# Four interleaved attention layers: VectorE may also take causal score banks

## The chip, the cores and the metric

One core of one Trainium2 chip. The metric is the device time of one execution, in microseconds (us); three executions of the kernel before are known, and one of another execution was recorded by the hardware profiler.

## The reference

Four residual layers on x of 2048 tokens by 512 features, all with 32 heads of 16 features. Layers 0 and 2 ("A") cut the tokens into four segments of 512: causal softmax attention inside each segment, blended by a gate with a read of a memory matrix that the earlier segments have filled. Layers 1 and 3 ("B") are plain attention of all tokens with all tokens.

```python
def _A_ref(x, wq, wk, wv, wo, beta):
    ...
    for s in range(N):                       # N = 4 segments, L = 512 tokens each
        qs, ks, vs = (q[:, :, s].copy(), k[:, :, s].copy(), v[:, :, s].copy())
        logits = jnp.einsum('bhqd,bhkd->bhqk', qs, ks) * scale + mask
        p = _softmax(logits, axis=-1)
        a_dot = jnp.einsum('bhqk,bhkd->bhqd', p, vs)
        pq = phi(qs)
        num = jnp.einsum('bhld,bhde->bhle', pq, M)
        den = jnp.einsum('bhld,bhd->bhl', pq, z)[..., None] + 1e-06
        a_mem = num / den
        o = g * a_mem + (1.0 - g) * a_dot
        outs.append(o)
        pk = phi(ks)
        M = M + jnp.einsum('bhld,bhle->bhde', pk, vs)
        z = z + jnp.einsum('bhld->bhd', pk)
    ...
def _B_ref(x, wqkv, wo):
    ...
    scores = jnp.einsum('bhqd,bhkd->bhqk', q, k) * Dh ** (-0.5)
    p = _softmax(scores, axis=-1)
    o = jnp.einsum('bhqk,bhkd->bhqd', p, v)
    ...
x = A_x
x = x + _A_ref(_layernorm(x, axis=-1), A_wq, A_wk, A_wv, A_wo, A_beta)
x = x + _B_ref(_layernorm(x, axis=-1), B_wqkv, B_wo)
x = x + _A_ref(_layernorm(x, axis=-1), A_wq, A_wk, A_wv, A_wo, A_beta)
x = x + _B_ref(_layernorm(x, axis=-1), B_wqkv, B_wo)
```

## The kernel before

The program is a list of instructions for each engine, made ahead of time by a planner (`Builder`) that walks through steps and keeps an estimate of each engine's time (`Sched`). What follows are the parts that the change and the prediction speak of.

**Banks.** PSUM has eight banks of 128 partitions by 512 fp32 values here. The scores of 128 keys (partitions) by 512 queries of one head fill one bank. In a B layer such a bank takes one matmul (32 rows of KB against a masked copy of the queries, `qm`); it is a full bank. In an A layer the causal triangle leaves ten blocks of 128 by 128 of a head's sixteen, packed in banks by `PARTS`: "k0" is one matmul of 512 columns, "k13" four matmuls of 128 columns (key blocks 1 and 3), and "k2" holds key block 2 of two heads. After the scores of a causal bank, one more matmul adds the mask: `ident` against `tri`, -1e9 above the diagonal, on 128 or 256 columns.

**Groups.** A group is a head in each of four rows of the array for one segment of queries. An A group has 12 banks (its first of a pair, e = 0) or 8 (its mate, e = 1, whose k2 blocks lie in the first's banks). A B group has 64 banks, or 16 or 32 where its keys come in waves. In all there are 640 causal banks and 4096 full ones.

**Units.** In each step `unit` scores the next three banks of the groups in the list `sel`, in order, into banks 0-2 or 3-5 in turn; one ScalarE activation (L1294) takes the exponential of all three into pT. The value matmuls ("pv") follow two units later and gather in bank 6. When all banks of a group are through, `finish` normalizes it (L1346, L1354).

**Bank 7** serves everything else: projections, output projections, the memory's matmuls, and the banks that VectorE takes.

**Taken banks.** In a step `dx_pick` may take one bank out of a group that is still to be scored. Its scores go to bank 7 and VectorE computes their exponential: L934 from PSUM into one half of a space "in" (dxt, later KA and QA too), then for a pair of banks at a time a chain of five instructions (L959, L962, L964, L966, L970) that ends in a space "out" (dxo, later VA too). Early there are two pairs of space in and three out. Once layer 0 is through (`dx_widen`, `self.wide`), its buffers make that four and four. The value matmuls read a taken bank from its out space when its group is the current one, and only then does the space come free. A bank is taken only if the group is a B one, of 64 banks unless much lies ahead (`NEARW`), has not yet given a sixth (wide: a fifth) of its banks, and if from the head of `sel` to its end at least 30 (wide: `REST` = 36) banks are left; a group ahead of the one that gives is shut. Further gates are: `near` (banks of all groups whose projections are done) not below `LOW` = 24; two units between takes, or more while other tasks wait (`ALT3` = 2, `ALT5` = 4); no projection half done; a free space in; bank 7 clear in time; VectorE not too late.

**Background.** Between units the planner runs tasks: layer norms, projections, memory updates, output projections, and the two chain tasks (`task_dx`), within a credit of VectorE time for each unit and while the estimates leave room. `dx_urgent` puts the chains first, and closes a half pair, when a group that has given banks has fewer than 30 (wide: `NEAR` = 24) left. If a group ends with a chain not through, `pv_step` runs the chain at once, in the middle of the unit. `evac` copies a projection out of bank 7 on VectorE, or on ScalarE if the estimate has VectorE more than 500 ns behind. `keep_busy` adds matmuls of zeros where the planner sees too little of TensorE's time in use.

**Order.** The work of layers 0 and 1 runs mixed, then 1 and 2, then 2 and 3: `select` puts a causal pair into `sel` behind the group at the head as soon as its projections are done, full groups behind it.

Of the kernel before, what the change touches and what calls it, by code (L numbers as in the profile page):

```python
# [255 lines left out]

class Builder:
    NPU = 4
    PHI_LATE = 100
    LAG_M = 2  # L260
    LOOK, PV_TAKEN = 1, 1
# [600 lines left out]
    def dx_pick(self, items):  # L862


        if self.low or self.near < self.PAIRS and len(self.dx_pairs) > self.PAIRS2 or self.step - self.dx_step < (2 - self.wide if not self.pending() else self.ALT3 if self.gap > 1 else self.ALT5) or self.cr_dve < -300 and self.late("dve") > self.EARLY or not self.dx_bufs or self.bank_late(self.unit_start()) > self.DX_BANK or self.late("dve") > (self.DX_FIN if self.ends(0) else self.DX_LATE):
            return None
        if any(t["next"][0][:1] == ["cont"] for t in self.tasks):
            return None
        used = {b[1] for _, b in items}
        rest = 0  # L870
        for n, g in enumerate(self.sel):
            rest += len(g.banks) - g.pos
            if g.kind != "B" or g.total < 64 and self.near < self.NEARW or g.shut or g.taken >= g.total // (self.TAKEN if self.wide else 6) or rest < (self.REST if self.wide else 30):
                continue
            for k in range(1, 9):
                if g.banks[-k][1] not in used:
                    bank = g.banks.pop(-k)
                    g.taken += 1
                    self.dx_step = self.step
                    for h in self.sel[:n]:  # L880
                        h.shut = True
                    return g, bank[0], bank[1]
        return None

    def pending(self):
        return any(t not in self.dx_tasks and self.met([n for n in t["next"][0] if n[0] != "at"]) for t in self.tasks)
# [62 lines left out]
    def dx_chain(self, k, b, ents):  # L949


        w = 512 * len(ents)
        ns = (690, 430, 1225) if len(ents) == 2 else (420, 295, 690)
        half = self.dx_space("in", b).bitcast(dt.uint16).rearrange("p (n two) -> p two n", two=2)
        lo, hi = half[:, 0, 0:w], half[:, 1, 0:w]
        z = self.dx_space("z", k)[:, 0:w]
        bt, bz = self.b_dxt[b], [self.b_dxz[k]]
        c = (350, 610, 1150) if self.wide else (440, 710, 1230)
        self.op("dve", lambda e: e.tensor_scalar(z, lo, EXP_K * 2.0 ** -16, EXP_K * EXP_F, op0=ALU.mult, op1=ALU.add), reads=bt,  # L959
                writes=self.dx_writes("z", k, self.b_dxz[k]), ns=ns[0])  # L960
        yield [], 0, c[1]
        self.op("dve", lambda e: e.tensor_tensor(z, z, z, ALU.mult), reads=bz, writes=bz, ns=ns[0])  # L962
        yield [], 0, c[0]
        self.op("dve", lambda e: e.tensor_scalar(z, z, EXP_B, EXP_A, op0=ALU.mult, op1=ALU.add), reads=bz, writes=bz, ns=ns[1])  # L964
        yield [], 0, c[1]
        self.op("dve", lambda e: e.tensor_tensor(z, z, z, ALU.mult), reads=bz, writes=bz, ns=ns[0])  # L966
        yield ["slot"], 0, c[2]
        slot = self.dx_free.pop(0)
        ob = self.dx_space("out", slot).bitcast(dt.int16)[:, 0:w]
        self.op("dve", lambda e: e.scalar_tensor_tensor(ob, hi, 128.0, z, op0=ALU.mult, op1=ALU.add), reads=bt + bz,  # L970
                writes=self.dx_writes("out", slot, self.b_dxo[slot]), ns=ns[2])
        self.dx_bufs.append(b)
        self.dx_now[k] = []
        self.dx_use[slot] = len(ents)
        for i, (g, what, r) in enumerate(ents):
            self.dxq.append((self.step + 2, g, what, r, slot, i))

    def later(self):
        return ("at", self.step + 1)
# [251 lines left out]
    def unit(self, n, items, dx):  # L1231
        u = n % 2
        al = self.new_alloc()
        slot = n % self.NPU
# [29 lines left out]
        if dx is not None:  # L1264
            g, what, r = dx
            bank7, al7 = self.misc(), self.new_alloc()
            rows = slice(32 * r, 32 * r + 32)
            ks, kk = self.kslot(g.L, what // 4), what % 4
            first_mm.append((self.ps[:, bank7.col0:bank7.col0 + 512], self.KB[rows, ks, g.c, kk * 128:(kk + 1) * 128],
                             self.qm[rows, g.qm, :], True, [self.b_KB[ks][g.c], self.b_qm[g.qm]], bank7, r, 512))  # L1270
        for (o, a, q, st, reads, bank, r, N) in first_mm + sum(second_mm, []):
            self.mm(o, a, q, st, True, reads, bank, al7 if dx is not None and bank is bank7 else al, tile=(32, 32 * r, 128, 0), n=N)
        for i, (g, (what, r)) in enumerate(items):
            if g.kind == "A":

                nb = 1 if what == "k0" else 2
                c0 = self.banks[3 * u + i].col0
                self.mm(bcast(self.ps[:, c0:c0 + 1], [[256, nb], [1, 128]]), self.ident[:, :], bcast(self.tri[:, 0:1], [[0, nb], [1, 128]]),
                        False, True, [self.b_ident, self.b_tri], self.banks[3 * u + i], al, n=128 * nb)
        if dx is not None:  # L1280
            self.dx_first(bank7, al7)
            self.dx_build.append(dx)
# [4 lines left out]
        i = 0  # L1287
# [248 lines left out]
```

## Time and profile before

| what | before |
|---|---|
| three executions | 1984.61, 1985.27, 1989.22 us (median 1985.27) |
| the profiled execution: time, span | 1984.7, 1983.0 us |
| granted TensorE clock, mean | 0.996 |
| ScalarE (ACT) busy, of it L1294 | 1933.0 us, 1904.8 us in 1407 instructions |
| VectorE (DVE) busy | 1654.2 us |
| TensorE (PE) busy, weight loads (PEld) | 1700.2 us, 933.7 us |
| banks taken by VectorE (L934) | 517 |

A busy time is the sum of an engine's instructions; matmuls overlap and their ends are modelled, so PE's share is not its share of peak. The slices are fortieths of the span in tenths of busy time. A group of instructions has its line, engine, operation, output<-input, shapes, count, busy time, mean duration, and the idle time of the engine just before them with what ended it. All matmuls have the line of the helper `mm`, so they are told apart by their tensors: ps<-qm,KB scores full banks, ps<-qm,KA causal ones, ps<-tri,ident is the mask, ps<-VB,pT and ps<-VA,pT are the value matmuls, ps<-wB,zero the matmuls of zeros. KA, QA and VA hold taken banks in the later part, beside what their names say.

### The profile page before, as it was taken

How to read it: one execution, taken by the hardware profiler on the slowest of the kernel's cores; microseconds unless marked ns; L12 is line 12 of the kernel's file. 1: busy time of each engine (PE TensorE's matmuls, PEld its weight loads, DVE VectorE, ACT ScalarE, POOL GpSimd, SP SyncE). 2: the span in 40 equal slices, each digit the busy share in tenths (PEclk: the TensorE clock that was granted, in tenths of full speed). 3: DMA queues.
4: the chain of work that ended last, by engine and by line, in shares of the span. 5: the costliest groups of instructions: out<-in, count | busy, mean ns of one | idle time of the engine just before them, and what ended most of it. 6: DMA issues, size and time to landing. Idle time of an engine off the chain costs nothing.

```text
span 1983.0 us, 61866 instructions
## 1 busy us (share of the span) xinstructions
PE 1700.2 (86%) x27320; PEld 933.7 (47%) x27734; DVE 1654.2 (83%) x2960; ACT 1933.0 (97%) x1447; POOL 89.1 (4%) x132
## 2 busy tenths in 40 slices
PE   8998888888888888888888889888888888888887
PEld 5554554444554445444454445444444444444444
DVE  5655554699899998899879996489999999999997
ACT  7999999999999999999999999999999999999998
POOL 0000001100000000000000000001000000000000
PEclk9999999999999999999999999999999999999999
DMA  5211111000100001100010011000000000000000
GB/s 155 37 21 34 28 23 23 4 10 18 18 7 15 5 15 24 15 15 8 18 21 13 5 25 23 12 4 7 15 5 4 5 15 5 5 7 15 5 5 12
DMA packets 100942, 34.82 MB, mean 18 GB/s; under 512 B 93504, under 2 KB 100160, under 8 KB 100672
## 3 DMA queue, kind: packets, MB, share of 16 engines
q1 hardware_dynamic: 100672, 30.83, 8.1%
q8 instruction: 217, 3.56, 0.8%
q14 instruction: 53, 0.43, 0.1%
HBM read 6.30 MB, written 2.10 MB: 4 GB/s over the span
## 4 chain that ended last, share of the span: by engine, by line
ACT 51%; issue 22%; PE 15%; DVE 9%; DMA 1%; SPq 0%; POOL 0%; ACTq 0%; DVEq 0%; POOLq 0%
ACT pT L1294 50%; PE ps L401 15%; ACT amem L620 1%; DVE dxo L970 1%; DVE dxt L934 1%; DVE ob L1354 1%; SPq L435 0%; DMA phq<-amem 0%; DVE VA L959 0%; DMA oT<-ob 0%; DVE VA L962 0%; DVE dxz L962 0%; DVE VA L970 0%; DVE dxz L959 0%; DVE VA L966 0%
## 5 line engine op out<-in xcount | busy, mean ns | idle before, releaser
L1294 ACT ACTIVATE pT<-ps 128x1536 bf16<-128x1536 f32 x1407 | 1904.8, 1619 | 33.8 <-PE ps L401 30.9
L401 PE MATMUL ps<-qm,KB 32*128 32x512 bf16 x4096 | 524.5, 385 | 196.5 <-ACT pT L1294 167.9
L401 PEld LDWEIGHTS ps<-VB,pT 128*128 128x128 bf16 x14316 | 459.9, 96 | 296.1 <-issue 217.7
L401 PE MATMUL ps<-VB,pT 128*128 128x34 bf16 (+1 forms) x14316 | 575.8, 186 | 19.9 <-DVE ob L1354 11.3
L401 PEld LDWEIGHTS ps<-qm,KB 32*128 32x128 bf16 x4096 | 133.8, 91 | 498.3 <-ACT pT L1294 445.6
L401 PE MATMUL ps<-wB,zero 128*128 128x512 bf16 x775 | 256.7, 379 | 10.2 <-issue 0.7
L934 DVE TENSOR_SCALAR dxt<-ps 128x512 uint32<-128x512 f32 x260 | 178.1, 685 | 19.6 <-PE ps L401 15.0
L1202 POOL TENSOR_SCALAR qm<-QB,par 128x512 bf16<-128x512 bf16 x86 | 81.5, 949 | 1741.2 <-PE ps L401 1459.9
L401 PE MATMUL ps<-qm,KA 32*128 32x128 bf16 (+2 forms) x1536 | 86.7, 254 | 25.8 <-ACT pT L1294 22.0
L401 PE MATMUL ps<-VB,dxo 128*128 128x51 bf16 (+1 forms) x1552 | 102.7, 186 | 0.9 <-DVE dxo L970 0.7
L401 PE MATMUL ps<-VA,pT 128*128 128x51 bf16 (+1 forms) x2560 | 101.0, 186 | 2.2 <-DVE ob L1354 1.5
L934 DVE TENSOR_SCALAR KA<-ps 128x512 uint32<-128x512 f32 x128 | 87.7, 685 | 11.0 <-PE ps L401 8.8
L401 PEld LDWEIGHTS ps<-VA,pT 128*128 128x128 bf16 x2560 | 92.0, 96 | 10.2 <-DVE ob L1354 5.0
L934 DVE TENSOR_SCALAR QA<-ps 128x512 uint32<-128x512 f32 x129 | 88.5, 686 | 8.0 <-PE ps L401 6.2
L401 PE MATMUL ps<-tri,ident 128*128 128x256 bf16 (+1 forms) x640 | 94.1, 255 | 0.0
L962 DVE TENSOR_TENSOR dxz<-dxz 128x1024 f16<-128x1024 f16 (+1 forms) x131 | 89.5, 683 | 0.7
L966 DVE TENSOR_TENSOR dxz<-dxz 128x1024 f16<-128x1024 f16 (+1 forms) x131 | 89.2, 681 | 0.4
L962 DVE TENSOR_TENSOR VA<-VA 128x1024 f16<-128x1024 f16 (+1 forms) x131 | 88.4, 675 | 0.6
L966 DVE TENSOR_TENSOR VA<-VA 128x1024 f16<-128x1024 f16 (+1 forms) x131 | 88.3, 674 | 0.5
L970 DVE SCALAR_TENSOR_TENSOR dxo<-dxt,dxz 128x1024 int16<-128x1024 uint16 (+1 forms) x66 | 80.6, 1221 | 0.2
L401 PEld LDWEIGHTS ps<-qm,KA 32*128 32x128 bf16 x1536 | 38.6, 92 | 86.6 <-ACT pT L1294 45.9
L970 DVE SCALAR_TENSOR_TENSOR dxo<-dxt,VA 128x1024 int16<-128x1024 uint16 (+1 forms) x66 | 78.7, 1192 | 0.2
(125 smaller groups left out, 1600.9 us busy)
## 6 DMA issues: line engine op xcount, KB each, us to landing
out_dram<-x SPq DMA_DIRECT2D x8, 256.0 KB, 2.1
x<-in_A_x_dram SPq DMA_DIRECT2D x3, 512.0 KB, 9.0
wB<-in_B_wqkv_dram SPq DMA_DIRECT2D x1, 1536.0 KB, 12.4
oT<-ob SPq DMA_TRANSPOSE x63, 2.5
xT<-xn SPq DMA_TRANSPOSE x60, 2.4
x<-in_A_x_dram SPq DMA_DIRECT2D x4, 128.0 KB, 2.2
wA<-in_A_wk_dram SPq DMA_DIRECT2D x1, 512.0 KB, 3.9
wA<-in_A_wq_dram SPq DMA_DIRECT2D x1, 512.0 KB, 5.0
```

The costliest lines, as they stand in the source:

```text
L401: self.sc.add("pe", lambda e: e.matmul(out, lhsT, rhs, start=start, stop=stop, skip_group_check=True), reads=reads, banks=[(bank, "w", all ...
L620: self.op("act", lambda e: e.activation(et, src, ACT.Exp), reads=bsrc, writes=self.b_amem, ns=1023, gap=915)
L934: self.op("dve", lambda e: e.tensor_scalar(d, o, SCALE * LOG2E * 65536, 126.0 * 65536, op0=ALU.mult, op1=ALU.add), writes=self.dx_writes(" ...
L962: self.op("dve", lambda e: e.tensor_tensor(z, z, z, ALU.mult), reads=bz, writes=bz, ns=ns[0])
L966: self.op("dve", lambda e: e.tensor_tensor(z, z, z, ALU.mult), reads=bz, writes=bz, ns=ns[0])
L970: self.op("dve", lambda e: e.scalar_tensor_tensor(ob, hi, 128.0, z, op0=ALU.mult, op1=ALU.add), reads=bt + bz, writes=self.dx_writes("out" ...
L1202: self.op(eng, (lambda m, q, col: lambda e: e.tensor_scalar(m, q, col, 0.0, op0=ALU.mult, op1=ALU.add))(m, q, col), reads=[bq, self.b_par] ...
L1294: self.sc.add("act", (lambda dst, src: lambda e: e.activation(dst, src, ACT.Exp, scale=SCALE))(dst, src), writes=self.b_pT[slot * 3 + i:sl ...
L1354: self.op("dve", lambda e: e.tensor_tensor(ob, src[:, :, 0:16], rb, ALU.mult), reads=[br] + bsrc, writes=[self.b_ob[oi][g.e]], bank=bk, al ...
```

## The change

`dx_pick` no longer skips causal groups. From an A group it may take the last bank that is not "k2" and whose row of the array no bank of this unit uses, if the group is not shut, has given fewer than two (`DXA`), at least 30 banks are near (`NEAR_A`; wide: `NEAR_AW` = 45), and at least 18 banks are left from the head of `sel` to its end (`REST_A`; wide: `REST_AW` = 20). `unit` scores such a bank into bank 7 by its `PARTS` and adds the mask matmul there. The common end of a take moves into a function, `dx_take`, and the lag before the value matmuls gets a name (`DXA_LAG` = 2, as for full banks).

```diff
 class Builder:
     NPU = 4
+    DXA, REST_A, REST_AW, DXA_LAG, NEAR_A, NEAR_AW = 2, 18, 20, 2, 30, 45
...
         for n, g in enumerate(self.sel):
             rest += len(g.banks) - g.pos
-            if g.kind != "B" or g.total < 64 and self.near < self.NEARW or g.shut or g.taken >= g.total // (self.TAKEN if self.wide else 6) or rest < (self.REST if self.wide else 30):
+            if g.kind == "A":
+
+                free = [k for k, b in enumerate(g.banks) if k >= g.pos and b[0] != "k2" and b[1] not in used]
+                if free and not g.shut and g.taken < self.DXA and self.near >= (self.NEAR_AW if self.wide else self.NEAR_A) and rest >= (self.REST_AW if self.wide else self.REST_A):
+                    return self.dx_take(g, g.banks.pop(free[-1]), n)
+                continue
+            if g.total < 64 and self.near < self.NEARW or g.shut or g.taken >= g.total // (self.TAKEN if self.wide else 6) or rest < (self.REST if self.wide else 30):
                 continue
             for k in range(1, 9):
                 if g.banks[-k][1] not in used:
-                    bank = g.banks.pop(-k)
-                    g.taken += 1
-                    self.dx_step = self.step
-                    for h in self.sel[:n]:
-                        h.shut = True
-                    return g, bank[0], bank[1]
+                    return self.dx_take(g, g.banks.pop(-k), n)
         return None
+
+    def dx_take(self, g, bank, n):
+        g.taken += 1
+        self.dx_step = self.step
+        for h in self.sel[:n]:
+            h.shut = True
+        return g, bank[0], bank[1]
...
-            self.dxq.append((self.step + 2, g, what, r, slot, i))
+            self.dxq.append((self.step + (self.DXA_LAG if g.kind == "A" else 2), g, what, r, slot, i))
...
             g, what, r = dx
             bank7, al7 = self.misc(), self.new_alloc()
             rows = slice(32 * r, 32 * r + 32)
-            ks, kk = self.kslot(g.L, what // 4), what % 4
-            first_mm.append((self.ps[:, bank7.col0:bank7.col0 + 512], self.KB[rows, ks, g.c, kk * 128:(kk + 1) * 128],
-                             self.qm[rows, g.qm, :], True, [self.b_KB[ks][g.c], self.b_qm[g.qm]], bank7, r, 512))
+            if g.kind == "A":
+                sl = self.aslot(g.L, g.qseg)
+                for m, (kb, off, N, q0) in enumerate(PARTS[what]):
+                    (second_mm[m - 1] if m else first_mm).append((
+                        self.ps[:, bank7.col0 + off:bank7.col0 + off + N], self.KA[rows, sl, g.c, kb * 128:(kb + 1) * 128],
+                        self.qm[rows, g.qm, q0:q0 + N], True, [self.b_KA[sl][g.c], self.b_qm[g.qm]], bank7, r, N))
+            else:
+                ks, kk = self.kslot(g.L, what // 4), what % 4
+                first_mm.append((self.ps[:, bank7.col0:bank7.col0 + 512], self.KB[rows, ks, g.c, kk * 128:(kk + 1) * 128],
+                                 self.qm[rows, g.qm, :], True, [self.b_KB[ks][g.c], self.b_qm[g.qm]], bank7, r, 512))
...
-        for i, (g, (what, r)) in enumerate(items):
+        for i, (g, (what, r)) in enumerate(items + ([(dx[0], dx[1:])] if dx is not None else [])):
             if g.kind == "A":
 
                 nb = 1 if what == "k0" else 2
-                c0 = self.banks[3 * u + i].col0
+                bank = self.banks[3 * u + i] if i < len(items) else bank7
+                c0 = bank.col0
                 self.mm(bcast(self.ps[:, c0:c0 + 1], [[256, nb], [1, 128]]), self.ident[:, :], bcast(self.tri[:, 0:1], [[0, nb], [1, 128]]),
-                        False, True, [self.b_ident, self.b_tri], self.banks[3 * u + i], al, n=128 * nb)
+                        False, True, [self.b_ident, self.b_tri], bank, al if i < len(items) else al7, n=128 * nb)
```

## The prediction

> **What bounds the kernel now.** I read the page first: engine shares, the 40 slices, the costliest groups.
>
> ```profile
> span 1983.0 us, 61866 instructions
> PE 1700.2 (86%) x27320; PEld 933.7 (47%) x27734; DVE 1654.2 (83%) x2960; ACT 1933.0 (97%) x1447; POOL 89.1 (4%) x132
> ...
> DVE  5655554699899998899879996489999999999997
> ACT  7999999999999999999999999999999999999998
> ...
> L1294 ACT ACTIVATE pT<-ps 128x1536 bf16<-128x1536 f32 x1407 | 1904.8, 1619 | 33.8 <-PE ps L401 30.9
> ...
> L934 DVE TENSOR_SCALAR dxt<-ps 128x512 uint32<-128x512 f32 x260 | 178.1, 685 | 19.6 <-PE ps L401 15.0
> ```
>
> ScalarE sets the time: 1407 exponentials of three banks take 1904.8 of 1983.0 us, and all its idle time is some 50 us. VectorE is the second exponential engine: L934 is the first step of each bank it takes, and its three groups (into dxt, KA and QA) are 260 + 128 + 129 = 517 banks. 1407 x 3 + 517 = 4738 answers to the 640 causal banks (one mask matmul each) and 4096 full ones (one qm,KB matmul each), the last units being short; the value matmuls that read taken banks are all of VB, so every taken bank was a full one. VectorE is full (9) in most slices, with holes at the left and at four places. Next I asked for the busy times in stretches chosen by two other views: the mask matmuls (tri, ident), which show when causal groups are scored (14-128, 185-208, 266-308, 519-557, 755-797, 1000-1041, 1193-1232 us), and the masked queries (qm from QA), which show when a causal pair enters the list `sel`, ahead of its scoring (171, 252, 494, 734, 973, 1185 us).
>
> ```profile
> 14.00:128.00 114.00, 105.17 (x1618) 62.20 (x1641) 70.88 (x189) 100.51 (x79) 0.00 (x0) 1.00 0.28 58
> 171.00:185.00 14.00, 10.96 (x177) 5.45 (x177) 7.22 (x29) 14.00 (x12) 0.00 (x0) 1.00 0.29 59
> 185.00:208.00 23.00, 21.05 (x333) 12.39 (x340) 11.36 (x24) 21.79 (x17) 2.63 (x4) 1.00 0.16 30
> ...
> 266.00:308.00 42.00, 37.96 (x648) 24.02 (x654) 22.31 (x45) 38.88 (x29) 2.34 (x4) 1.00 0.16 26
> ...
> 505.00:519.00 14.00, 12.77 (x207) 7.72 (x208) 8.40 (x12) 14.00 (x12) 0.00 (x0) 1.00 0.15 29
> ...
> 755.00:810.00 55.00, 46.19 (x799) 28.47 (x805) 42.50 (x79) 50.32 (x39) 3.35 (x6) 0.97 0.15 26
> ...
> 984.00:1000.00 16.00, 14.36 (x225) 8.42 (x226) 7.42 (x13) 16.00 (x13) 0.00 (x0) 1.00 0.09 18
> 1000.00:1042.00 42.00, 34.99 (x654) 23.19 (x659) 36.40 (x69) 40.87 (x32) 3.96 (x4) 1.00 0.13 21
> ...
> 1193.00:1232.00 39.00, 36.59 (x634) 23.70 (x638) 25.12 (x49) 37.25 (x29) 2.86 (x9) 1.00 0.11 22
> 1400.00:1600.00 200.00, 170.61 (x2779) 87.13 (x2821) 194.88 (x308) 198.91 (x149) 13.69 (x8) 0.99 0.03 7
> ```
>
> Columns: stretch, length, busy time of PE, PEld, DVE, ACT, POOL, granted clock, DMA share, GB/s. In 1400-1600 VectorE is 97% busy: no room. Around every causal stretch ScalarE is full while VectorE is 35 to 85% busy. The same view for L934 alone says how many banks were started:
>
> ```profile
> 505.00:519.00 14.00, 0.00 (x0) 1.00 0.15 29
> ...
> 984.00:1000.00 16.00, 0.17 (x1) 1.00 0.09 18
> 1000.00:1042.00 42.00, 6.02 (x9) 1.00 0.13 21
> ...
> 1400.00:1600.00 200.00, 56.29 (x82) 0.99 0.03 7
> ```
>
> 82 banks in 200 us when VectorE is fed; one in the 30 us of the two stretches before a causal wave. There `dx_pick` finds nothing: the full group at the head has under REST (36) banks left, and behind it stand only causal groups, which it skips. In the first 370 us none is taken at all: the groups there are causal, or full ones of 16 banks, barred by NEARW.
>
> **What a bank is worth, and costs.** On ScalarE: 1904.8 / 1407 / 3 = 0.451 us off the bounding engine. On VectorE in a pair: 0.685 (L934) plus half of 0.685 + 0.689 + 0.418 + 0.687 + 1.217 (L959, L962, L964, L966, L970), 2.53 us. A causal group has 12 or 8 banks, always under NEAR, so `dx_urgent` closes its pair early and many causal banks go alone. The trace's few 512-wide chains show 0.42 for L959 and 0.69 for L970; with about 0.4, 0.3 and 0.4 for the middle, scaled from the wide rows, 2.9 us. This costs nothing where VectorE has the time shown above.
>
> **How many banks, late part (wide).** The window of a pair: at rest >= 20 (REST_AW) the second of a pair qualifies while the group ahead still runs, the first too if that has 8 left or more; once the pair itself is at the head neither does. A projection under way bars a take, and bank 7 must be clear. 505-519 has 10 units, and takes come at best every second unit with projections pending: 3. 984-1000: 12 units, 4. In 734-755 six are already taken: 1. Inside the four causal stretches full groups behind were already drawn on (13 takes in 519-557, 13 in 755-810, 9 in 1000-1042), so a causal bank mostly replaces a full one there. Yet a full bank taken ahead holds its output space until its group's turn (4 slots of 2): in 755-810 L934 goes on while L970 stops from 781.5 to 806.4 us. A causal bank frees its slot soon: 1, 3 and 2 more. In 1193-1232 two were taken and 13.9 us are free, but few banks stand ahead there, against the floor of 45: 3. Sum 17; by free VectorE time the bound is about 53 us / 2.9 = 18; I take 12, since each take needs bank 7 between two projections. Bounds 4 and 18.
>
> **Early part.** Counting pairs whose projections are through, less banks scored, the banks ahead are 5 to 55 in 14-128 us and 33 to 106 later, so the floor of 30 bars about half of 14-128 and little after. Takes are four units apart while projections wait. 171-185 and 252-266 (10 units each): 5 together. 185-208 and 266-308 (46 units, six pairs, one take in each): 6. In 14-128 some 4, but there ScalarE is idle 13.5 us of 114, TensorE is 92% busy and the projections set the pace, so I count half. Sum 11 + 2 = 13, bounds 5 and 22.
>
> **TensorE.** The score pieces and the mask matmul of a taken bank move from banks 0-5 to bank 7, and its four value matmuls read dxo instead of pT: the same instructions, nothing in sum. A projection behind the take waits for bank 7, about 0.7 us; in the late windows it is hidden by full-group scoring that lasts until 519 and 1000 us, and uncovered it would be 0.7 x 25 = 17 us at the very most. `DXA_LAG` is 2, as the literal was: nothing. Pulling `dx_take` out of the loop: nothing.
>
> **Losses.** (a) A VectorE busier in these phases pushes an evacuation to ScalarE where the planner sees it 500 ns behind; the one of KA there took 0.63 us. I take 2; bounds 0 and 8. (b) The reciprocal and multiply that close a group (0.25 + 0.42 us) queue behind chain steps of up to 1.2 us; the value matmuls of the next group wait for bank 6. ScalarE holds one more unit (1.33 us), which covers one such step: 0 to 3 us, I take 1. (c) A taken causal bank must be through before its group ends: below.
>
> **The clock.** Four stretches of 3.413 us ran at half clock; the first:
>
> ```profile
> 800.96:804.37 3.41, 1.55 (x36) 0.90 (x33) 2.73 (x6) 3.15 (x3) 0.00 (x0) 1.00 0.00 0
> 804.37:807.78 3.41, 3.41 (x32) 1.50 (x32) 1.90 (x2) 1.45 (x1) 0.00 (x0) 0.50 0.57 47
> ```
>
> In it two gaps between exponentials were 2.78 and 2.61 us instead of 1.33, 2.7 us lost; the three others lost 1.1 to 1.3 us each. TensorE had been 45 to 69% busy in the 3.41 us before. One dip more or less is +-1.5 us, and a stall of some microseconds could bring one: -3 to +6 us, I take 0. The Trainium skill ("TensorE: Matmul & The Clock Gate", part 1) has the clock fall after at least one idle window of about 3.4 us; by it no dip would be added, as nothing here leaves TensorE idle that long. The trace does not agree: 1.55 to 2.34 us busy did not keep the clock.
>
> **Sum.** 12 + 13 = 25 banks x 0.451 = 11.3 us off; 2 x 0.63 and 1 us back, and 1 us for late banks: 8 us. The profiled execution took 1984.7 us (span 1983.0 and 1.7 around it), 0.6 below the median of 1985.27. 1984.7 - 8 + 0.6 = 1977 us. By the bounds: 40 banks and no loss give -18 (1967 us); 9 banks (4.1), against 5 + 3 + 6 us of (a), (b) and dips, give +10 (1995 us).
>
> **Rivals.**
> 1. *Substitution.* Causal banks only take the place of full ones: the steps between takes, bank 7 and the credit per unit give the rate, not the candidates. For it: 6 and 13 takes in 734-755 and 755-810 with VectorE not full. Against it: none in 505-519, none before 370. Under 12 more banks: -5 to +3 us, about 1983 us.
> 2. *Late banks, slower.* From L934 to the end of L970 the banks held in KA and QA took 5.1 us at least and 17 to 19 us at the median, since chains queue in order of their pairs. A causal bank taken at rest 18 to 20 is due 6 to 7 units later, plus two of lag: 11 us. If full pairs stand ahead, the group's end forces the chain in the middle of the unit: TensorE's queue waits at the value matmul, the next scores stand behind it, and ScalarE has 1.33 us in hand. At 1.5 us of ScalarE per late bank, half of 25 late is 12 x 1.5 = 18 us against 11 gained: 1985 + 7 = 1992 us. It decides from 7 late banks on. For it: 11 us lies between minimum and median. Against it: urgent chains go ahead of the projections, and before 370 us and in 505-519 and 984-1000 no full pairs queue; 5.1 us is the latency there.
> 3. *Nothing happens:* rest 18 or 20 against 12 + 8 banks passes only with a group still ahead, and so few pass that under 6 banks move: 1984 us. Taken with 1.
>
> Chances: forecast 0.50; substitution or nothing 0.31; late banks or another stall 0.19. About 0.3% (6 us) is what a measurement of this kernel can tell from no change; the forecast and the part of its range below 1979 are faster, rivals 1 and 3 the same, rival 2 slower: 0.50, 0.31, 0.19. The range goes from just under the lower bound, 1966, over rival 2 to the upper bound, 1995. For the forecast alone it is 1967 to 1979.
>
> **What would show it.** L1294 falls from 1407 to about 1398 or 1399, L934 rises from 517 to about 542, with L934 rows in 14-370 us and matmuls of VA with dxo; VectorE's left slices rise from 5 to 6. What TensorE and its weight loads wait for dxo, 0.9 + 1.3 us now, stays under 10 us; above 20 rival 2 holds. L934 under 530 in all means rival 1. I am wrong if ScalarE's count falls as said and the time doesn't: then the gain went into new idle time before L1294, 33.8 us now.

## The result, and the profile after

The kernel after took 2013.08 us (median of four runs, 2011.87 to 2014.27) against 1985.36 before: a ratio of 1.0141 [1.0128, 1.0153]. It is slower by 28 us; the forecast was 1977. Its page, the same rows as before:

```profile
span 2012.4 us, 62396 instructions
PE 1764.7 (88%) x27756; PEld 940.0 (47%) x27756; DVE 1689.9 (84%) x3067; ACT 1932.4 (96%) x1449; POOL 85.1 (4%) x126
...
DVE  5667664599989997899889885469999999999997
ACT  7889998999999999999999997999999999999998
...
L1311 ACT ACTIVATE pT<-ps 128x1536 bf16<-128x1536 f32 x1405 | 1902.8, 1630 | 57.3 <-PE ps L402 54.7
...
L943 DVE TENSOR_SCALAR dxt<-ps 128x512 uint32<-128x512 f32 x271 | 186.0, 686 | 24.9 <-PE ps L402 20.9
```

L1311 is the former L1294, L943 the former L934, L402 the former L401. VectorE does fill its holes (slices 3 to 6 rise from 5 to 6 or 7). PE's 1764.7 us against 1700.2 is no measure of a change: the trace of before holds 27320 matmuls to 27734 weight loads, so 414 of its matmuls aren't recorded; in after none is missing. But ScalarE's work stays where it was, 1932.4 us against 1933.0, with 1405 exponentials instead of 1407, and the span less that work, ScalarE's idle time, goes from 50.0 to 80.0 us. The idle time before L1311 that TensorE ends carries 23.8 us of it.

To see where, I counted the score banks in the order in which TensorE issued them (the qm,KB matmuls and the mask matmuls, 4736 in each kernel) and took the time at which the n-th was issued, less that of before; beside it ScalarE's idle time up to then and the taken banks up to then, both less those of before (the banks are counted from 0).

```
n-th score bank         100   200   500   800  1100  1400  2700  2800  4700
issued at, before (us)   70   128   268   404   524   642  1175  1224  1957
after: later by (us)    3.1   3.3   3.6   5.1   4.9  15.1  17.5  30.9  29.5
ScalarE idle, more      2.5   4.4   6.8   9.0  10.5  18.6  18.9  30.9  30.0
taken banks, more         1     2     9    10    16    12    11    10    10
```

At the end the sum closes: 30.0 us more idle time and 0.6 us less work of ScalarE (exponentials 2.0 less, four more evacuations 2.4 more, the rest is where instructions overlap) are the 29.4 us between the spans. Three steps carry the loss: the first 800 banks, 1100 to 1400, and 13.4 us inside banks 2700 to 2800. From there on nothing is lost.

### The profile page after: what moved, and what is told of

It reads as the page before. It is cut to its first block, busy times and chain, and to the rows that moved or that the text cites. A ratio compares the mean times of both kernels' runs of the same rounds, so it can differ in the third digit from the quotient of the medians.

```text
span 2012.4 us, 62396 instructions
## 1 busy us (share of the span) xinstructions
PE 1764.7 (88%) x27756; PEld 940.0 (47%) x27756; DVE 1689.9 (84%) x3067; ACT 1932.4 (96%) x1449; POOL 85.1 (4%) x126
## 4 chain that ended last, share of the span: by engine, by line
ACT 51%; issue 22%; PE 18%; DVE 8%; DMA 1%; POOL 0%; ACTq 0%; SPq 0%; DVEq 0%; POOLq 0%
ACT pT L1311 50%; PE ps L402 18%; DVE dxo L979 1%; ACT amem L621 1%; DVE ob L1371 1%; DVE VA L971 0%; DVE dxt L943 0%; DVE VA L968 0%; DMA oT<-ob 0%; DVE KA L943 0%; DVE VA L979 0%; DVE rd L1363 0%; DVE VA L975 0%; DVE VA L429 0%; DVE dxz L975 0%
## 5 line engine op out<-in xcount | busy, mean ns | idle before, releaser
L1311 ACT ACTIVATE pT<-ps 128x1536 bf16<-128x1536 f32 x1405 | 1902.8, 1630 | 57.3 <-PE ps L402 54.7
L402 PE MATMUL ps<-qm,KB 32*128 32x512 bf16 x4096 | 520.6, 386 | 180.6 <-ACT pT L1311 149.3
L402 PEld LDWEIGHTS ps<-VB,pT 128*128 128x128 bf16 x14412 | 465.4, 96 | 288.1 <-issue 215.8
L402 PE MATMUL ps<-VB,pT 128*128 128x51 bf16 (+1 forms) x14412 | 580.4, 186 | 18.1 <-DVE ob L1371 13.6
L402 PEld LDWEIGHTS ps<-qm,KB 32*128 32x128 bf16 x4096 | 132.8, 91 | 519.4 <-ACT pT L1311 460.9
L402 PE MATMUL ps<-wB,zero 128*128 128x512 bf16 x1102 | 351.4, 381 | 0.0
L943 DVE TENSOR_SCALAR dxt<-ps 128x512 uint32<-128x512 f32 x271 | 186.0, 686 | 24.9 <-PE ps L402 20.9
L979 DVE SCALAR_TENSOR_TENSOR dxo<-dxt,VA 128x1024 int16<-128x1024 uint16 (+1 forms) x109 | 130.9, 1201 | 0.3
L402 PE MATMUL ps<-qm,KA 32*128 32x128 bf16 (+2 forms) x1536 | 95.1, 255 | 20.7 <-ACT pT L1311 12.9
L402 PE MATMUL ps<-VA,pT 128*128 128x51 bf16 (+1 forms) x2424 | 96.9, 187 | 3.3 <-DVE ob L1371 2.6
L402 PE MATMUL ps<-VB,dxo 128*128 128x34 bf16 (+1 forms) x1492 | 98.8, 186 | 1.1 <-DVE dxo L979 0.8
L402 PE MATMUL ps<-tri,ident 128*128 128x256 bf16 (+1 forms) x640 | 97.5, 257 | 0.0
L943 DVE TENSOR_SCALAR KA<-ps 128x512 uint32<-128x512 f32 x129 | 88.6, 687 | 9.7 <-PE ps L402 6.8
L943 DVE TENSOR_SCALAR QA<-ps 128x512 uint32<-128x512 f32 x127 | 87.2, 686 | 9.7 <-PE ps L402 7.4
L402 PEld LDWEIGHTS ps<-VA,pT 128*128 128x128 bf16 x2424 | 87.2, 96 | 14.7 <-DVE ob L1371 7.1
L971 DVE TENSOR_TENSOR dxz<-dxz 128x1024 f16<-128x1024 f16 (+1 forms) x145 | 92.6, 639 | 1.0
L975 DVE TENSOR_TENSOR dxz<-dxz 128x1024 f16<-128x1024 f16 (+1 forms) x145 | 92.3, 636 | 0.9
L971 DVE TENSOR_TENSOR VA<-VA 128x1024 f16<-128x1024 f16 (+1 forms) x136 | 90.9, 669 | 1.0
L975 DVE TENSOR_TENSOR VA<-VA 128x1024 f16<-128x1024 f16 (+1 forms) x136 | 91.0, 669 | 0.5
L968 DVE TENSOR_SCALAR VA<-dxt 128x1024 f16<-128x1024 uint16 (+1 forms) x125 | 84.7, 678 | 0.8
L402 PEld LDWEIGHTS ps<-qm,KA 32*128 32x128 bf16 x1536 | 43.0, 92 | 78.5 <-ACT pT L1311 33.6
```

Of the source, the lines that this page charges most:

```text
L402: self.sc.add("pe", lambda e: e.matmul(out, lhsT, rhs, start=start, stop=stop, skip_group_check=True), reads=reads, banks=[(bank, "w", all ...
L943: self.op("dve", lambda e: e.tensor_scalar(d, o, SCALE * LOG2E * 65536, 126.0 * 65536, op0=ALU.mult, op1=ALU.add), writes=self.dx_writes(" ...
L1311: self.sc.add("act", (lambda dst, src: lambda e: e.activation(dst, src, ACT.Exp, scale=SCALE))(dst, src), writes=self.b_pT[slot * 3 + i:sl ...
```

## The theory, and its rivals

*Theory A, order.* A bank more or less shifts which task the planner puts into which unit; somewhere list or projections then come out of step, and TensorE has nothing ready for ScalarE. What is lost hangs on the place, not on the number of banks.
*Theory B, VectorE.* Its added chains delay work for which TensorE waits, and the loss grows with the causal banks.
*Theory C, late banks.* A taken causal bank isn't through when its group ends, and TensorE waits for its output (dxo). This is the prediction's rival 2.

The runs in one table (causal: banks taken from A groups; exps: exponentials; idle: the span less ScalarE's busy time; these columns are of the profiled execution, which in e4 and e5 lies 4.8 and 2.4 us above the median):

```
kernel                median  ratio to before           taken (causal)  exps  idle
before               1985.36                              517  (0)       1407  50.0
after                2013.08  1.0141 [1.0128, 1.0153]     527 (34)       1405  80.0
e1_early_only        1998.48  1.0068 [1.0053, 1.0083]     525 (10)       1405  63.8
e2_late_only         2002.66  1.0092 [1.0077, 1.0107]     511 (23)       1409  63.0
e3_ghost             1994.39  1.0049 [1.0032, 1.0065]     497 full ones  1402  65.4
e13_late_ghost       1987.89  1.0016 [1.0007, 1.0026]     494 full ones  1406  54.2
e4_wait_for_v        2006.68  1.0115 [1.0100, 1.0130]     521 (36)       1407  76.4
e5_first_two         2001.62  1.0091 [1.0076, 1.0106]     519  (2)       1407  68.3
e9_two_wait_v        1991.27  1.0036 [1.0022, 1.0049]     519  (2)       1407  54.5
e10_late_projection  1992.26  1.0041 [1.0028, 1.0055]     517  (0)       1407  57.0
e6_early_rest        1986.71  1.0016 [1.0006, 1.0025]     523  (6)       1406  54.6
e7_control           1991.33  1.0037 [1.0024, 1.0051]     508  (0)       1410  52.6
e8_reshuffled        1999.94  1.0080 [1.0065, 1.0095]     521 (32)       1407  65.8
e14_late_queries     2000.69  1.0078 [1.0063, 1.0093]     511 (23)       1409  60.2
e11_fallback         1985.92  1.0004 [0.9995, 1.0012]     521 (12)       1405  54.0
e12_before_limits    1986.70  1.0014 [1.0005, 1.0023]     516  (0)       1407  49.9
```

## Experiments 1 and 2: each half alone

```diff
-    DXA, REST_A, REST_AW, DXA_LAG, NEAR_A, NEAR_AW = 2, 18, 20, 2, 30, 45
+    ... = 2, 18, 20, 2, 30, 1000000000      # e1: none once layer 0 is through
+    ... = 2, 18, 20, 2, 1000000000, 45      # e2: none before
```

> Causal banks are taken only until layer 0 is through (NEAR_AW out of reach, 10 such takes). Theory A, the losses are separate stalls of TensorE, each in its own place: by bank 800 of the scores this is about 5 us behind before, as the change is, and what follows depends on where projections then meet the groups; 1990 to 2000 us. Theory B, VectorE's extra work (a single chain for nearly every causal bank) is the loss: 10 of 34 banks, in a phase with VectorE half idle, cost little; 1983 to 1988 us. Theory C, banks that are late at the end of their group: no more waits for dxo than before here, so no loss; 1982 to 1986 us.

> Causal banks are taken only after layer 0 is through (NEAR_A out of reach). Theory A: the first 374 us are as before; what is lost later depends on whether a causal wave again meets its own unfinished value projections (13 us in the change at 1214 us); without that 1990 to 1998 us, with it 2000 to 2008 us. Theory B: nearly the whole loss stays, 2005 to 2012 us, because 23 of the takes are late ones and VectorE is full there. Theory C: waits for dxo of 5 us or more, 2000 to 2010 us.

Early alone lost 13.5 us with 10 causal banks, late alone 17.6 us with 23; each half loses. In e2 the count itself turned: 488 full banks and 23 causal ones, six fewer than before in all. e1 has only four half-clock stretches, as many as before (after has ten), so its loss isn't the clock's; its time lies in A's range. e2 fits no theory as it was put: it is above A's 1990 to 1998 us for an order without a forced value projection (ScalarE's longest wait in its late part up to 1990 us is 2.89 us, shown below), and below B's 2005.

C gets no support. In e2 TensorE and its weight loads waited 0.4 and 1.1 us for dxo, where C asked for 5. In e1 it was 5.1 and 7.9 us (0.9 and 1.3 in before), but 10.8 of these 13.0 us came after 1500 us, where ScalarE waited only 2.2 us for TensorE.

## Experiments 3 and 4: the bank without VectorE's work

```diff
         if dx is not None and dx[0].kind == "A":
+            self.dxq.append((self.step + 2, *dx, -1, 0))    # picked, not scored
+            dx = None
...                                                          # in pv_taken
+            if slot < 0:
+                self.pv(g, what, r, Fixed(self.ident[:, :]), self.b_ident)
+                continue
```

e13_late_ghost is the same with e2's limit.

> The same rule picks causal banks, but a picked bank is left out: it is not scored and VectorE does nothing for it; its value matmuls read the identity matrix in its place. So the 34 or so banks are free for ScalarE, VectorE and bank 7. Theory B or C (VectorE's chains or their lateness are the loss): about 34 x 0.451 = 15 us faster than before, 1968 to 1975 us. Theory A (the early end of causal groups disturbs what TensorE meets in the middle of a unit, and ScalarE runs short of banks, whoever computes them): no gain, 1983 to 1995 us, with ScalarE's idle time above 60 us against 50 before.

> The late causal banks alone, as in the run with late takes, but a picked bank is left out: not scored, no work on VectorE, its value matmuls read the identity matrix. Theory B for the late part (VectorE's chains and what queues behind them cost): about 1972 to 1985 us, that is 17 us or more below the run with the work. Theory A for the late part too (the order alone): 1995 to 2003 us.

Even with the causal banks' scores and exponentials gone (such a bank is a ghost below), ScalarE was idle 15.4 us more than before (e3) and the kernel was slower than before. A loss therefore needs neither VectorE's chains (B) nor late banks (C), nor a bank scored into bank 7. Full banks fell to 497 and 494 though VectorE had less to do (1614.7 and 1606.4 us busy): causal picks displace full ones without taking VectorE's time. That is substitution, shown. That the spacing of the picks does it is likely, but not shown: a change of order alone can cost full banks too (nine in e7, below).

The late half speaks in part for B: e13 lies between the two ranges, nearer to B's, and e2 lies 14.8 us above it in the medians. Of the 15.9 us between their spans 8.8 are idle time and 7.1 ScalarE's own work; some 4 of the 7.1 are only the count, as e13 has 520 banks off ScalarE (26 left out, 494 taken) and e2 511. Their orders differ too, from 503 us on. One stretch of e2 shows how VectorE comes in (the timeline; square brackets hold the idle time before and what ended it):

```profile
546.69 1.10 DVE L971 TENSOR_TENSOR dxz<-dxz 128x1024 f16<-128x1024 f16 x1
547.71 1.21 DVE L979 SCALAR_TENSOR_TENSOR VA<-QA,VA 128x1024 int16<-128x1024 uint16 x1
548.85 0.60 DVE L1211 TENSOR_SCALAR qm<-QA,par 128x512 bf16<-128x512 bf16 x2
...
549.50 0.60 PE L402 MATMUL ps<-qm,KA 32*128 32x128 bf16 x4 [2.65 <-DVE qm L1211]
...
550.64 1.45 ACT L1311 ACTIVATE pT<-ps 128x1536 bf16<-128x1536 f32 x1 [2.89 <-PE ps L402]
```

The masked queries of a causal pair are VectorE's too, small instructions at the end of a queue of chain steps; TensorE stands for them, and ScalarE behind it. The table of waits of before, then of after (total, count, longest):

```profile
PEld ps L401 <- DVE qm L1202: 3.0, 3, 1.6
PE ps L401 <- DVE qm L1202: 2.1, 2, 1.1
```

```profile
PEld ps L402 <- DVE qm L1211: 12.4, 12, 2.1
PE ps L402 <- DVE qm L1211: 8.5, 10, 1.8
PEld ps L402 <- DVE dxo L979: 2.8, 6, 1.1
PE ps L402 <- DVE dxo L979: 1.8, 3, 1.0
```

The weight loads' and the matmuls' waits stand beside each other, so TensorE waits 6 to 9 us longer for queries. In e13, which leaves the chains of the causal banks out, both rows are 3.0 and 2.1 us as in before. What TensorE waits for dxo is small in after too. But the queries' wait alone doesn't give the price: e8 (below), 12 us faster than after, waits longer for them (16.2 and 11.5 us), and e3, which leaves the chains of the causal banks out, still 7.4 and 5.7.

The second step of after, banks 1100 to 1400, goes with waits for VectorE as well. The waits of ScalarE, and of TensorE for the closing of groups (ob), in after (529 to 658 us), then in before (524 to 643 us):

```profile
ACT pT L1311 <- PE ps L402: 8.2, 10, 2.0
PE ps L402 <- DVE ob L1371: 3.6, 6, 1.1
```

```profile
ACT pT L1294 <- PE ps L401: 0.2, 1, 0.2
PE ps L401 <- DVE ob L1354: 0.4, 2, 0.2
```

With masked queries (1.8 us), a chain's last step into VA (1.6) and dxo (1.0) TensorE waited 8.0 us for VectorE there, 0.6 in before. No run separates these waits from the order in which they arose.

## Experiment 5: can that wait be taken away?

```diff
-                eng = "dve" if late or isA or any(h.kind == "A" for h in self.sel) else "pool"
+                eng = "dve" if late or isA and not self.wide or any(h.kind == "A" for h in self.sel) else "pool"
```

With e2's limit.

> The late causal banks alone, with the masked queries of causal groups made on GpSimd in the late part instead of VectorE, so that TensorE no longer waits for them behind chain steps. If that wait is a good part of the late loss: 1993 to 1998 us instead of 2002.7, and the stall of 2.9 + 1.25 us at 548 us gone. If not: 2000 to 2005 us.

Inconclusive: only 5 of the 64 causal query operations went to GpSimd, TensorE ran the same instructions in the same order as in e2, and the waits stayed at 10.2 and 6.1 us (9.6 and 6.1 in e2). How much of the late 14.8 us the queries alone cost stays open.

## Experiment 6: the 13 us at 1214 us

Here ScalarE of the kernel after, then TensorE:

```profile
1211.50 2.96 ACT L1311 ACTIVATE pT<-ps 128x1536 bf16<-128x1536 f32 x2
1218.21 0.60 ACT L427 ACTIVATE VA<-ps 128x512 bf16<-128x512 f32 x1 [3.75 <-PE ps L402]
1222.63 1.45 ACT L1311 ACTIVATE pT<-ps 128x1536 bf16<-128x1536 f32 x1 [3.83 <-PE ps L402]
```

```profile
1212.50 1.03 PE L402 MATMUL ps<-wA,xT 128*128 128x512 bf16 x4
1214.71 1.04 PE L402 MATMUL ps<-wA,xT 128*128 128x512 bf16 x4 [1.19 <-DVE VA L429]
1216.53 1.64 PE L402 MATMUL ps<-wA,xT 128*128 128x512 bf16 x4 [0.79 <-DVE VA L429]
1218.86 1.89 PE L402 MATMUL ps<-wA,xT 128*128 128x512 bf16 x4 [0.69 <-ACT VA L427]
1220.54 0.70 PE L402 MATMUL ps<-VA,pT 128*128 128x34 bf16 x12
```

The causal pair enters the list as soon as its keys and queries are there, and is scored at once (its queries left bank 7 at 1206.5 us, the first scores came at 1208.4). Two units later come its value matmuls, and no value projection of the segment is done. So the planner runs all four in the middle of the unit, one after another through bank 7, each waiting for the evacuation of the one before: 8.2 us without an exponential, 7.6 of them idle. In before the four were done between 1185 and 1195 us, beside other units. The cure would be a pair that waits for its values:

```diff
-            return [("K", g.L, g.qseg, g.c), ("Q", g.L, g.qseg, g.c)]
+            return [("K", g.L, g.qseg, g.c), ("Q", g.L, g.qseg, g.c)] + ([("V", g.L, g.qseg)] if g.L and g.qseg == 3 else [])
```

> As the change, but the causal groups of layer 2's last segment are let into the list only when their value projections are issued too, so that no value matmul there has to run four projections in the middle of a unit. Theory A: the 13 us lost at 1214 us (bank 2700 to 2800) go, and the rest stays: 2000 to 2005 us. Theories B and C: nothing of the sort is their cause; 2010 to 2014 us.

Between banks 2700 and 2800 the loss of 13.4 turned into a gain of 4.8 us, and ScalarE runs through:

```profile
1206.79 26.16 ACT L1311 ACTIVATE pT<-ps 128x1536 bf16<-128x1536 f32 x19
```

Up to 1208 us TensorE's instructions and their order are the same in both kernels, so this shows the cause. But in the new order behind the edit 13 us were lost again between 2800 and 3000, with six fewer taken banks and 6.6 us of idle time, so the kernel gained only 6.4 and missed the range of A by 1.7 us. The pair also shows how far two executions of one order can lie apart: between banks 400 and 500 e4 lost 5.2 us, after 1.6. e4 had half-clock stretches at 73.7, 230.7 and 240.9 us, where after had none. So a step of some 5 us or less in these tables isn't shown by one pair of traces. After's early loss is safer: e1, e4, e5, e8 and e9, which share its order up to bank 200, are 3.2 to 4.9 us late there too. The next pair of runs repeats the test on a smaller case.

## Experiments 7 and 8: two causal banks in the whole program

```diff
-                if free and not g.shut and g.taken < self.DXA and ...
+                if free and not g.shut and self.step < 60 and g.taken < self.DXA and ...
```

e9_two_wait_v adds the wait of experiment 6 for the first segment of layer 2 (`g.qseg == 0`); TensorE's order is that of e5 up to 523 us.

> Causal banks are taken only before unit 60: two in the whole program. Theory A, now sharper: the costs do not scale with the banks, since a bank that leaves a group changes which unit every later projection and group change falls in, and the order before has no value projection in the middle of a unit and few waits for masked queries, while a shifted order has; 3 us lost at once at 70 us, and 5 to 15 us later; 1992 to 2002 us. Theory B or C (a price for each bank): two banks cost or bring at most 2 us, 1984 to 1988 us.

> As the run with two causal banks, but the causal groups of layer 2's first segment enter the list only when their value projections are issued. The two banks, all 519 takes and the early order are the same. Theory A: the 16 us that two banks cost between bank 1100 and 1200 are value projections forced into the middle of a unit, and go; 1988 to 1993 us instead of 2001.6. If the 16 us have another cause (VectorE, the clock alone): 1998 to 2003 us.

```
n-th score bank         100   200   500  1100  1200  1400  2700  2800  4700
e5: later by (us)       3.4   4.3   5.1   1.8  18.1  19.0  13.2  20.7  19.1
e9: later by (us)       3.1   3.3   3.7  -0.5  -0.1   5.5   4.5   5.7   5.5
```

Two causal banks, at 39 and 96 us, cost 17.6 us: more than the 23 of e2 per bank by an order of magnitude. Most of it is lost 400 us later, where not one causal bank is taken. ScalarE of e5 there:

```profile
524.59 4.68 ACT L1311 ACTIVATE pT<-ps 128x1536 bf16<-128x1536 f32 x3
532.99 0.60 ACT L427 ACTIVATE VA<-ps 128x512 bf16<-128x512 f32 x1 [3.72 <-PE ps L402]
534.83 1.45 ACT L1311 ACTIVATE pT<-ps 128x1536 bf16<-128x1536 f32 x1 [1.25 <-PE ps L402]
537.75 1.45 ACT L1311 ACTIVATE pT<-ps 128x1536 bf16<-128x1536 f32 x1 [1.46 <-PE ps L402]
```

It is the same trap in another segment, and in e9, with the same 519 taken banks, the step of 16.3 us between banks 1100 and 1200 is 0.4 us. Theory A holds here: two banks taken before 100 us decide whether values are projected in time at 530 us.

## Experiments 9 and 10: no causal bank at all, and the other six

The first take, in unit 14, keeps a projection out of bank 7. e10 does only that, for one unit, in the kernel before; e6 takes the early causal banks from unit 60 on.

```diff
-  self.step == self.dx_step or ...
+  self.step in (self.dx_step, 14) or ...                          # e10, in before
-  if free and not g.shut and g.taken < self.DXA and ...
+  if free and not g.shut and 60 < self.step and g.L == 0 and g.taken < self.DXA and ...   # e6, in after
```

> No causal bank is taken: the kernel before, with the projection of unit 14 held off for one unit, as bank 7 holds it when a causal bank is taken there. Theory A: the first 3.5 us that the change loses at 70 us come from that late projection and not from the bank; here too about 3 us are lost by bank 100, and 1986 to 1992 us in all. If the bank's own work is the cause: 1983 to 1985 us and nothing lost by bank 100.

> The other early banks alone: causal banks of layer 0 from unit 60 on (6 takes). Theory A: an order that happens to meet no such place costs little; 1984 to 1990 us, well below what two banks cost in the run beside it. Theory B or C: 6 banks cost three times as much as two.

One projection held back by one unit cost 8.2 us without a single causal bank. I had expected 3 us by bank 100; there it was 0.1. The 3.1 us that after loses by then are one evacuation more on ScalarE (0.6) and 2.5 us of idle time: at 72.1 us an output projection waited 1.70 us for VectorE's addition of the one before (L802), which came behind small instructions of a layer norm and two masked queries. Nor is e10's delay all of after's: the two projection matmuls whose weights before loads at 39.1 us come at 40.1 in e10 and, three units late, at 43.1 in after. Whether the bank or its longer delay brings those 3.1 us stays open. The 8.2 us came later: 2.1 by bank 200, 2.8 by 300, 8.7 by 400, and nothing from there to the end. Before and e10, the same stretch:

```profile
172.00:225.00 53.00, 45.82 (x710) 25.44 (x720) 26.09 (x67) 51.79 (x40) 4.80 (x10) 1.00 0.20 37
```

```profile
172.00:225.00 53.00, 44.95 (x676) 25.41 (x684) 21.71 (x53) 47.05 (x36) 3.46 (x5) 0.94 0.18 29
```

Four fewer ScalarE instructions in 53 us, and a granted clock of 0.94: two half-clock stretches (184 and 205 us) that before doesn't have. How much of the loss these two make isn't traced. What had moved by then is the order of the projections: the queries of the third segment's second pair leave bank 7 at 159.7 us instead of 109.9 (141.9 in after). In after the list itself runs dry at 120.5 us, where ScalarE waits while eight projection matmuls pass with no unit beside them:

```profile
123.52 0.60 ACT L427 ACTIVATE VB<-ps 128x512 bf16<-128x512 f32 x1 [3.04 <-PE ps L402]
```

The six other early banks (e6) cost 2.7 us. Here the count came out as summed: six more taken, and ScalarE's work fell by 2.4 us to 1930.6 (6 x 0.451 = 2.7). But its idle time rose by 4.6 us, in small pieces without a stall of note.

## Experiments 11 and 12: how much does a shuffle of the order cost by itself?

`DVE_LATE` bars a take when VectorE is this many ns late. e7 is before with 1180 instead of 1200, e8 is after with 1220.

```diff
-    DX_BANK, DX_LATE, BG_BANK, DVE_LATE, DVE_LATE_LOW = 500, 4000, 200, 1200, 5000
+    DX_BANK, DX_LATE, BG_BANK, DVE_LATE, DVE_LATE_LOW = 500, 4000, 200, 1180, 5000   # e7; 1220 in e8
```

> No causal bank is taken at all: the kernel before with one neutral limit of the planner moved by 20 ns (DVE_LATE 1180 for 1200). Theory A: any other order of the same work costs something, because the old constants fit the old order; 1988 to 1995 us. If the loss needs causal banks: 1984 to 1987 us.

> The change with the same limit moved the other way (DVE_LATE 1220): 32 causal banks, 521 in all, in another order. Theory A: the part of the loss that is one order's bad luck (the stall at 1214 us above all) goes, the rest stays; 1996 to 2004 us. Theory B or C: as the change, 2010 to 2015 us.

20 ns in a limit, with no causal bank, cost before 7.4 us: nine fewer taken banks, so three exponentials more (ScalarE works 3.4 us longer), and 2.6 us of idle time, all after bank 2000. The other way, 20 ns took after from 28 us over before to 16, with 32 causal banks. So 12 of the 28 us are the particular order into which the change fell; 16 remain in e8.

## Experiments 13 and 14: a better version?

If causal banks displace full ones, they may be taken only where no full one is to be had. e11 does that, with limits chosen for it; e12 is before with two limits changed: ALT5 as in e11, and CR_A, which e11 leaves alone. So it shows what moved limits can do without causal banks; it isn't e11 less its rule.

```diff
-                    return self.dx_take(g, g.banks.pop(free[-1]), n)
+                    back = g, free[-1], n            # the first such; taken at the end of the loop if no full bank came
...
+    DXA 3, REST_A 24, REST_AW 24, NEAR_A 60, NEAR_AW 100, MARGIN 500, DX_BANK 400, CR_B 1400, ALT5 5    # e11
+    CR_A 1350, ALT5 5                                                                                  # e12
```

> A gentler version: a causal bank only where no full bank is to be had (DXA 3, REST_A 24, REST_AW 24, NEAR_A 60, NEAR_AW 100), with four limits moved (CR_B 1400, MARGIN 500, DX_BANK 400, ALT5 5) so that its order meets few bad places; 12 causal banks, 521 in all. Theory A: banks that come on top of the full ones, in an order without forced projections, bring 0.45 us for each bank more: 4 banks, 1982 to 1985 us. Theory B: 12 single chains cost, 1988 us or more.

> Its counterpart without causal banks: the kernel before with two limits moved (CR_A 1350, ALT5 5), 516 takes. Theory A: as fast as the version with 12 causal banks or faster, 1981 to 1985 us: what a causal bank brings is no more than what an order brings.

e11 equals before within 0.12% either way: its four more taken banks took 2.3 us off ScalarE (1930.7 us busy), and 4.0 us of idle time came back. e12 gained nothing either. Both lie 1 to 2 us above the ranges that A gave them. No version was faster than before.

## Why the prediction was wrong, point by point

- **The bound.** Right: ScalarE sets the time, and every microsecond of the loss is ScalarE's idle time or its own work. That this idle time stays as it was when the order changes was taken for granted; it is the step that failed (50.0 us became 80.0).
- **How many banks.** 25 more, with L943 at 542: wrong, 10 more and 527. The 34 causal banks are above the 25, but full ones fell from 517 to 493. Rival 1's mark (under 530) was met, and the ghosts show that causal picks displace full ones; its price (-5 to +3 us) missed the rest. I had reckoned substitution only inside the causal stretches; after them 6 of the 16 banks won by bank 1100 were given back.
- **0.451 us a bank.** Ten banks should be 3.3 exponentials; two went, as three are now short instead of one. What came off ScalarE's exponentials is 2.0 us (1904.8 to 1902.8), not 11.3. An exponential that stands alone takes 1.45 us in the profile, one in an unbroken row some 1.37 (16 of them 22.09), and their waits for TensorE went from 62 to 88.
- **VectorE's price.** 2.9 us for a single and "this costs nothing": VectorE did 35.7 us more for 10 more banks, as chains of one bank rose from 7 to 35. The holes were free in the mean, but not at the moments when the masked queries were due: 6 to 9 us of waiting. That wait isn't in the sum; the text named the queue behind a chain only for the closing of a group (loss b, 1 us). For that TensorE waited 16.1 us against 13.4, so 2.7 us more.
- **TensorE, "A projection behind the take waits for bank 7, about 0.7 us".** This is the mis-sized term, which the sum put at nothing. Behind the first take the projection came 4.0 us late (43.1 for 39.1 us), three units on, and what hangs on it (which pair is ready, when values are projected) moves: 8.2 us for a projection held by a single unit in e10, and with two takes another 16.3 us through the values at 530 us (e5 against e9). The uncovered bound of 17 us was for all 25 together.
- **Losses.** (a) Two more evacuations on ScalarE: four, 2.4 us. (c) and rival 2, late banks: wrong mechanism. TensorE and its loads waited 2.8 + 1.8 us for dxo; with the chain's last step into VA, 1.7 + 1.6 us, it is 7.9, under the 10 us that spoke against it. The side that it stood for, slower, came by another stall.
- **The clock, taken at 0.** Ten half-clock stretches instead of four, with 16.3 us of ScalarE's idle time in them or within a microsecond of them (4.4 before); since the stalls above lie there too, that is no separate price. The Trainium skill ("TensorE: Matmul & The Clock Gate", part 1) has the clock fall after an idle window of about 3.4 us. No run here agrees: in the seven traces with no matmul missing TensorE was busy 1.06 to 2.75 us of the 3.41 before a dip (second ones in a row left out), and others of these windows passed without one with 1.71 to 1.99 us. The prediction's 1.55 to 2.34 us are lower bounds, as the trace of before lacks matmuls.
- **"I am wrong if ScalarE's count falls as said and the time doesn't".** The idle time before L1294 went from 33.8 to 57.3 us: the place named was the right one, while the count fell by 2, not by 8.

What stays open: how the late 17.6 us divide between the waits for VectorE, the displaced full banks and the order. Early and late make 31 us alone and 28 together, so the parts don't add.

## What to carry to other kernels

In a program whose order is planned ahead and then fixed, an edit that moves one item also moves everything planned after it; the price per item times items is then the smaller term. Before trusting such a sum, look up what is ready only just in time (here the values of a pair and its masked queries), and run a control that changes the order and nothing else: here 20 ns in a limit are worth 7 to 12 us, as much as the gain forecast. When more candidates are offered to a stage, ask first what sets its rate; where it isn't the number of candidates, the new ones displace the old.

## What the runs showed of the hardware

The half clock needs no idle TensorE, and the busy time before it isn't a clean threshold: 2.75 us of 3.41 brought one in e7 (607 us), 1.71 us brought none in after (73.4 us), and 1.72 us in the same place brought one in e5 (72.9 us), whose TensorE order is that of after up to 151 us. I had not expected a stall of 3.75 us on ScalarE to go with two such stretches in a row: at 1216.8 us, after 3.4 us with TensorE busy for 1.4, projections that otherwise take 1.03 us for four matmuls took 1.64 and 1.89.
